# A decode step bound by its loads: one row block of the last weight matrix loaded first of all

## The chip, the cores and the metric

The kernel runs on one core of one Trainium2 chip. The metric is the device time of one execution in microseconds (us); lower is better. Names used below: PE is the matrix engine (TensorE), DVE the vector engine, ACT the scalar engine, POOL the general one (GpSimd), SP the engine that issues nearly all DMAs here.

## The reference

One token goes through a block of attention over a long key and value cache and then through a mixing and feed-forward block.

```
x  [1,1,512], wq [512,4096], k_cache, v_cache [1,8,16384,128], wo [4096,512]
w1, w2 [512,512], w3 [512,1792], w4 [1792,512]

h  = x + A(layernorm(x), k_cache, v_cache, wq, wo)
     A: q = x @ wq as 32 heads of 128, four heads to each of 8 key heads
        p = softmax(q k^T / sqrt(128)),  o = p v,  result = o @ wo
out = h + B(layernorm(h), w1, w2, w3, w4)
     B: h1 = gelu(layernorm(x) @ w1); its four quarters are shifted along the
        sequence by +1, -1, +2, -2 with zeros shifted in; hs = shifted @ w2
        x1 = x + hs
        result = x1 + gelu(layernorm(x1) @ w3) @ w4
```

The sequence has one position, so each shift leaves zeros only: hs is zero, w1 and w2 do not matter, and the kernel does not load them. Everything is bfloat16.

## The kernel before

All that the kernel reads is streamed from HBM once, 79 MB, by DMAs that SP issues one after another on one queue (line 458, the helper `load`). The order is: the query weights wq (4 MB, into the buffer vb), the first two halves of the keys (4 MB each, into the two halves of kb), the values of the first pair (8 MB, into vb), and then for three more pairs of key heads the two key halves and the values. Then come wo in two pieces (`WO`, blocks 0 to 20 and 20 to 32), w3 in one (`W3`) and w4 in three (`W4`). A buffer is loaded again as soon as its last reader is done: SP waits for the transposes of the keys (DVE, line 635) or for the matmuls with the values (PE, line 686), and then issues. Only the tiny load of x goes by ACT's queue.

The start: x is normalised (lines 579 to 602); DVE's cast xn (line 603) also waits for wq; 32 matmuls (line 612) make the queries; DVE spreads them (lines 619 and 626). The first value load waits for these matmuls, since it overwrites wq.

Each of the four pairs of key heads: DVE transposes both key halves into kt (line 635), PE multiplies them with the queries (line 646), DVE and ACT do the softmax (lines 660 to 675), PE multiplies with the values (line 686), DVE and PE gather the result (lines 702 to 710). While the softmax runs, PE is given matmuls that nobody reads (line 498).

The end: the product with wo (line 755), the sum with x and its row sums (lines 767, 512 to 524), the product with w3 (line 780), the gelu in two halves on ACT (line 792), two transposes on DVE that lay its result out as hcol (line 796), and the product with w4 (line 803). w4 is [1792, 512]; the kernel sees it as 14 row blocks, block m being rows m, 14+m, 28+m and so on over 128 partitions, 512 columns (1 KB) to a partition, so a block is 128 KB. For each block PE does four matmuls of 128 columns, 56 in all, into one accumulator. The pieces are blocks 0 to 7, 8 to 12, and 13 alone. The first matmul that needs a piece waits for it, except that the wait for the first piece is put on the first transpose of line 796. The first half of hcol holds blocks 0 to 6, the second blocks 7 to 13. DVE and ACT then copy one half of the result each (lines 810 and 811), and SP stores it (line 813).

The order of work on each engine is the order in which the program is written; nothing reorders it. Between engines, a class that records every operation (lines 25 to 89) works out from the tiles read and written which semaphore each operation waits for.

Of the kernel before, what the change touches and what calls it, by code (L numbers as in the profile page):

```python
# [7 lines left out]
BF16 = mybir.dt.bfloat16  # L8
# [333 lines left out]
D = 512  # L342
# [8 lines left out]
NHC = FM // 128  # L351
# [2 lines left out]

SEEN, ROUND = 47, 28
W3 = ((0, 4),)
W4 = ((0, 8), (8, 13), (13, 14))
PAIRS = HKV // 2
RPARTS = 6
QPAD = 4 * 7  # L360
# [10 lines left out]
def bass_sequential_preLN__gqa_block_cached__mixer_s_mlp__decode_kernel(  # L371
# [13 lines left out]
    with ExitStack() as ctx:  # L385
        sb = lambda name, shape, dt: ctx.enter_context(nc.sbuf_tensor(name, shape, dt))
# [50 lines left out]
        hg = sb("hg", [128, FQ], BF16)  # L437
        hT = sb("hT", [128, NCH, 32], FP32)
        hcol = sb("hcol", [128, NHC, 32], BF16)
        fin = sb("fin", [64, 256], BF16)  # L440
        kb_all = sb("kb", [128, 256 * DH], BF16)
        kb = [kb_all[:, i * 128 * DH:(i + 1) * 128 * DH] for i in range(2)]
# [4 lines left out]
        w4_sb = kb[1][:, NCH * FM:2 * NCH * FM].rearrange("p (m c) -> p m c", m=NHC)  # L447
# [9 lines left out]
        def load(name, dst, src, key, by="SP", also=()):  # L457
            P.op(by, lambda e: e.dma_start(dst, src), w=[key, *also], dma=name)  # L458
# [33 lines left out]
        def pe(fn, r=(), w=(), bank=(), also=(), times=None, many=1):  # L492

            return P.op("PE", fn, r, w, bank, also=also, times=times, many=many)
# [6 lines left out]
        def piece(cuts, m):  # L501
            return [lo <= m < hi for lo, hi in cuts].index(True)
# [42 lines left out]
        def inverse_roots(i, ns):  # L545
# [9 lines left out]
            for m in range(3):  # L555
# [5 lines left out]
                else:  # L561
# [2 lines left out]
                        r=[(S, 8)], w=[(T, k + n) for k in (0, 2) for n in ns])  # L564


        load("x4", x4[:, :], A_x[0, 0:1, :].rearrange("o (q j) -> (o q) j", q=4), "x4", "ACT")
        load("wq", wq_sb[:, 0:NCH * HQ * DH], A_wq.rearrange("(p k) c -> p (k c)", k=NCH), ("v", 0), also=[("v", x) for x in range(1, VP)])
        load_keys(0, 0)
# [10 lines left out]
            r=["ident_f", "x4"], w=["quarter"])  # L580
        pe(lambda e: e.matmul(O_ps[0][:, 0:128], quarter[:, :, :].rearrange("p q u -> p (q u)"), x4[:, :],  # L581
                              start=True, stop=True), r=["quarter"], w=[("O", 0)], bank=[("O", 0)])
# [9 lines left out]
            r=["ident_f"], w=["row32"])  # L592
        dve(lambda e: e.tensor_reduce(maskdd[:, :], ident_f[:, :].rearrange("p (n d) -> p d n", d=4), AX.X, ALU.add),
            r=["ident_f"], w=["maskdd"])
# [3 lines left out]
        for z, src, key, of, n in ((zo, row32[:, :].rearrange("p (g n h) -> p g h n", g=2, h=REP), "zo", "row32", 4),  # L598
# [6 lines left out]
            r=["hT", (("st", 0), 0), (("st", 0), 6)] + [("v", x) for x in range(VP)], w=["xn"])  # L605
# [3 lines left out]
        for i, key in enumerate(keys):  # L609
            P.part("query", i)  # L610
            for k in range(NCH):
                pe(lambda e, k=k: e.matmul(row[:, bass.ds(P.b + P.b0, 512)], copies(xn[:, k:k + 1], 128),  # L612
                                           wq_k[:, k, bass.ds(P.c + P.c0, REP * DH)], start=(k == 0), stop=(k == NCH - 1)),
                   r=["xn"], also=[("v", x) for x in range(VP)], w=["n" if key == "mn" else key], bank=[key])
        P.part()
        for g in range(2):
            half = banks[64 * g:64 * g + 64, PAIRS * g:PAIRS * g + PAIRS, :].rearrange("p j c -> p (j c)")
            for b in range(2):
# [3 lines left out]
                    r=["n" if x == "mn" else x for x in keys[PAIRS * g:PAIRS * g + PAIRS]], w=["qcol"],  # L622
# [118 lines left out]
        w3_in = B_w3.rearrange("(p k) f -> p k f", p=128)  # L741
        for n, (lo, hi) in enumerate(W3):
            load(f"w3{n}", w3_sb[:, lo:hi, :], w3_in[:, lo:hi, :], ("r", 1, n))
        w4_in = B_w4.rearrange("(p m) c -> p m c", p=128)
        for n, (lo, hi) in enumerate(W4):
            load(f"w4{n}", w4_sb[:, lo:hi, :], w4_in[:, lo:hi, :], ("r", 1, len(W3) + n))

# [2 lines left out]
            r=["o_m"], w=["o_f"])  # L750
        dve(lambda e: e.tensor_copy(o_b[:, :], o_f[:, :]), r=["o_f", ("r", 0, 0)], w=["o_b"])  # L751

        for r_ in range(32):
# [3 lines left out]
                                              stop=(r_ < 4 or r_ >= 28), skip_group_check=(r_ >= 4)),  # L757
               r=["o_b"] + [("r", 0, n) for n in (piece(WO, r_),) if n], w=[("O", 0)], bank=[("O", 0)],
# [3 lines left out]
        h_ps, hkey = banks[:, 6, :], "spare0"  # L762
        for n in range(2):
            dve(lambda e, n=n: e.tensor_copy(osum[:, 256 * n:256 * n + 256], O_ps[0][:, 256 * n:256 * n + 256]),
                r=[("O", 0)], w=[("osum", n)], bank=[("O", 0)])
        for q in range(4):
            pe(lambda e, q=q: e.matmul(h_ps[32 * q:32 * q + 32, 0:128], copies(row32[:, 0:1], 32),
                                       osum[:, q * 128:(q + 1) * 128], start=True, stop=True),
               r=[("osum", q // 2), "row32"], w=[hkey], bank=[hkey])
# [4 lines left out]
            r=["hT", (S, 0)] + [("r", 1, 0)], w=["hc"])  # L774
# [3 lines left out]
        for k in range(NCH):  # L778
            for q in range(4):
                pe(lambda e, k=k, q=q: e.matmul(s_ps[32 * q:32 * q + 32, 0, 0:FQ], hc[:, k, :],  # L780
                                                w3_sb[:, k, q * FQ:(q + 1) * FQ], start=(k == 0), stop=(k == NCH - 1)),
                   r=["hc"] + [("r", 1, n) for n in (piece(W3, k),) if n], w=[("s", 0)], bank=[("s", 0)])
# [6 lines left out]
            r=["xs", (S, 6), "hr"], w=[hkey], bank=[hkey])  # L789
        for n in range(2):  # L790
# [5 lines left out]
            dve(lambda e, lo=lo, hi=hi: e.transpose(  # L796
                hcol[:, lo:hi, :].rearrange("p m u -> p (m u)"),
                hg[:, :].rearrange("p (i m) -> p m i", m=NHC)[:, lo:hi, :]), r=[("hg", n)] + [("r", 1, len(W3))] * (n == 0), w=[("hcol", n)])
        for m in range(NHC):
            if m == 4:  # L800
                pe(None)
            for o in range(4):
                pe(lambda e, m=m, o=o: e.matmul(
                    h_ps[32 * o:32 * o + 32, 0:128], hcol[:, m, :], w4_sb[:, m, o * 128:(o + 1) * 128],
                    start=False, stop=(m == NHC - 1), skip_group_check=True),
                   r=[("hcol", 2 * m // NHC)] + [("r", 1, len(W3) + n) for n in (piece(W4, m),) if n],
                   w=[hkey], bank=[hkey])


# [5 lines left out]
             r=[("fin", 0), ("fin", 1)], w=["out"], dma="out")  # L815
# [32 lines left out]
```

## Time and profile before

| What | Value |
|---|---|
| Median of 3 runs | 189.83 us (189.8 to 189.89) |
| The profiled execution | 189.74 us |
| Its span, first to last instruction | 188.4 us |
| PE, DVE busy | 127.9 us (68%), 116.8 us (62%) |
| ACT, POOL busy | 13.7 us (7%), 4.6 us (2%) |
| SP's DMA queue, share of the 16 engines' span | 97.9% |
| Bytes read from HBM | 79.17 MB, 420 GB/s over the span |

Durations below come from the profiled execution. Its time is the span and some 1.3 us around it. How to read the rows: the profile's page has a line for each resource with the span cut into 40 equal slices, a digit giving the busy share in tenths. In a timeline a row is start, duration, engine, line, operation, tiles and shape, number of instructions, and in brackets the idle time before it and what ended that. In a table of windows, each engine has its busy time and in brackets how many of its instructions touch the window; the last three columns are the granted PE clock, the DMA engines' busy share and GB/s. A DMA packet is counted in the window in which it starts. SP's rows give only the issuing; when a load lands is told by the table of issues, as time from issue to landing.

### The profile page before, as it was taken

How to read it: one execution, taken by the hardware profiler on the slowest of the kernel's cores; microseconds unless marked ns; L12 is line 12 of the kernel's file. 1: busy time of each engine (PE TensorE's matmuls, PEld its weight loads, DVE VectorE, ACT ScalarE, POOL GpSimd, SP SyncE). 2: the span in 40 equal slices, each digit the busy share in tenths (PEclk: the TensorE clock that was granted, in tenths of full speed). 3: DMA queues.
4: the chain of work that ended last, by engine and by line, in shares of the span. 5: the costliest groups of instructions: out<-in, count | busy, mean ns of one | idle time of the engine just before them, and what ended most of it. 6: DMA issues, size and time to landing. Idle time of an engine off the chain costs nothing.

```text
span 188.4 us, 2405 instructions
## 1 busy us (share of the span) xinstructions
PE 127.9 (68%) x767; PEld 49.6 (26%) x767; DVE 116.8 (62%) x139; ACT 13.7 (7%) x21; POOL 4.6 (2%) x8
## 2 busy tenths in 40 slices
PE   0109705979699059796980697969829997885772
PEld 0104201423225024232240242322413332222221
DVE  5740799795451897944518979445279897513173
ACT  3000200000040000000400000003000000500012
POOL 8100000000000000000000000000000000000000
PEclk9999985899999859999998599999988999999999
DMA  6999999999799999999999999997999989899994
GB/s 223 445 445 445 445 417 473 445 445 445 334 445 445 445 501 417 390 390 417 445 445 445 445 445 445 445 445 334 445 445 445 556 390 417 362 393 424 435 411 177
DMA packets 2751, 79.19 MB, mean 420 GB/s; under 512 B 318, under 2 KB 446, under 8 KB 574
## 3 DMA queue, kind: packets, MB, share of 16 engines
q1 hardware_dynamic: 2742, 79.17, 97.9%
q8 instruction: 1, 0.02, 0.0%
q10 hardware_dynamic: 8, 0.00, 0.0%
HBM read 79.17 MB, written 0.00 MB: 420 GB/s over the span
## 4 chain that ended last, share of the span: by engine, by line
DMA 36%; DVE 29%; PE 29%; issue 4%; SPq 0%; DVEq 0%
DVE kt L635 24%; DMA kb<-in_A_k_cache_dram 15%; DMA kb<-in_B_w_dram 15%; PE banks L646 13%; DMA vb<-in_A_wq_dram 7%; PE banks L498 6%; PE banks L612 5%; PE banks L686 4%; DVE mx L660 1%; DVE od L705 1%; DVE qcol L619 1%; PE banks L663 1%; PE banks L708 0%; SPq L458 0%; DVE od L702 0%
## 5 line engine op out<-in xcount | busy, mean ns | idle before, releaser
L646 PE MATMUL banks<-kt,qn 128*128 x256 | 68.8, 409 | 26.8 <-DVE kt L635 26.0
L635 DVE STREAM_TRANSPOSE kt<-kb 128x4096 int32<-128x4096 int32 (+2 forms) x25 | 70.7, 2878 | 5.4 <-PE banks L646 4.0
L646 PEld LDWEIGHTS banks<-kt,qn 128*128 x256 | 26.0, 102 | 69.1 <-issue 53.1
L498 PE MATMUL banks<-qb 128*128 128x512 bf16 x70 | 25.5, 388 | 0.6
L686 PE MATMUL banks<-vb,pt 128*32 128x512 bf16 x256 | 14.7, 379 | 0.9 <-POOLq L480 0.9
L671 ACT ACTIVATE p_sb<-banks,bias 128x1024 bf16<-128x1024 f32 x4 | 4.5, 1114 | 132.7 <-DVE nmh L667 132.7
L660 DVE TENSOR_REDUCE mx<-banks 128x1 f32<-128x1024 f32 x4 | 4.9, 1225 | 14.2 <-PE banks L646 14.2
L675 DVE STREAM_TRANSPOSE pt<-p_sb 64x1024 bf16<-64x1024 bf16 x8 | 9.9, 1239 | 5.4 <-ACT p_sb L671 5.3
L612 PE MATMUL banks<-vb,xn 128*128 x32 | 8.6, 436 | 6.8 <-DVE xn L603 6.8
L498 PEld LDWEIGHTS banks<-qb 128*128 128x128 bf16 x70 | 6.7, 97 | 18.3 <-issue 18.1
L702 DVE TENSOR_SCALAR od<-banks,rowc 128x128 f32<-128x128 f32 x4 | 1.4, 351 | 14.4 <-PE banks L686 14.4
L686 PEld LDWEIGHTS banks<-vb,pt 128*32 128x32 bf16 x256 | 8.5, 97 | 5.1 <-POOLq L480 1.0
L619 DVE STREAM_TRANSPOSE qcol<-banks 64x1024 f32<-64x1024 f32 x4 | 4.8, 1227 | 6.8 <-PE banks L612 6.8
L612 PEld LDWEIGHTS banks<-vb,xn 128*128 128x128 bf16 x32 | 3.5, 110 | 11.4 <-issue 8.7
L663 PE MATMUL banks<-mxd,mean 128*128 128x128 f32 x8 | 2.0, 326 | 6.6 <-DVE mxd L661 6.6
L708 PE MATMUL banks<-od,zo 128*32 128x128 f32 x8 | 1.6, 285 | 6.5 <-DVE od L705 6.5
L655 ACT ACTIVATE banks<-mean 128x1024 f32<-128x1024 f32 x4 | 4.1, 1027 | 18.7 <-DVE qcol L619 18.6
L695 DVE RECIPROCAL den<-banks 32x1 f32<-32x1 f32 x4 | 0.6, 156 | 6.9 <-PE banks L693 6.9
L705 DVE SCALAR_TENSOR_TENSOR od<-banks,rowc,od 128x128 f32<-128x128 f32 x12 | 4.2, 351 | 0.4
L755 PE MATMUL banks<-kb,o_b 128*32 128x512 bf16 x44 | 3.3, 384 | 1.6 <-DVE o_b L751 1.1
L581 PE MATMUL banks<-x,quarter 4*128 4x128 bf16 x1 | 0.3, 283 | 5.5 <-DVE quarter L579 5.5
L579 DVE CAST quarter<-ident_f 4x128 bf16<-4x128 f32 x1 | 3.2, 3224 | 1.0 <-DMA x<-in_A_x_dram 1.0
(69 smaller groups left out, 39.6 us busy)
## 6 DMA issues: line engine op xcount, KB each, us to landing
kb<-in_A_k_cache_dram SPq DMA_DIRECT2D x8, 4096.0 KB, 27.8
vb<-in_A_wq_dram SPq DMA_DIRECT2D x1, 4096.0 KB, 12.3
kb<-in_A_wo_dram SPq DMA_DIRECT2D x1, 2560.0 KB, 26.1
kb<-in_B_w_dram SPq DMA_DIRECT2D x1, 1792.0 KB, 24.2
kb<-in_A_wo_dram SPq DMA_DIRECT2D x1, 1536.0 KB, 29.4
kb<-in_B_w_dram SPq DMA_DIRECT2D x1, 1024.0 KB, 26.3
kb<-in_B_w_dram SPq DMA_DIRECT2D x1, 640.0 KB, 27.4
kb<-in_B_w_dram SPq DMA_DIRECT2D x1, 128.0 KB, 27.3
```

What stands on the lines that cost most here:

```text
L498: P.op("PE", lambda e: e.matmul(O_ps[1][:, :], field[:, 0:128], field[:, 0:512], start=True, stop=True), r=["qb"], bank=[("O", 1)], times= ...
L612: pe(lambda e, k=k: e.matmul(row[:, bass.ds(P.b + P.b0, 512)], copies(xn[:, k:k + 1], 128), wq_k[:, k, bass.ds(P.c + P.c0, REP * DH)], sta ...
L619: dve(lambda e, g=g, b=b, half=half: e.transpose(qcol[64 * g:64 * g + 64, 2 * b:2 * b + 2, :, :].rearrange("p e m u -> p (e m u)"), half.r ...
L635: P.op("DVE", lambda e, view=view: e.transpose(view(kt), view(kb[y])), r=[("r", y, i) for i in range(RPARTS)], w=[("kt", t + i) for i in r ...
L646: pe(lambda e, n=n: e.matmul(row[:, bass.ds(P.y, 512)], qn[:, n, bass.ds(P.q, 128)], key_piece(P.k, n), start=False, stop=(n == 3), skip_g ...
L655: act(lambda e: e.activation(s_all, copies(mean4[:, 0:1], 1024), ACTF.Identity, scale=0.0), r=["mean4", "p"], w=[("s", 0), ("s", 1)], **both)
L660: dve(lambda e: e.tensor_reduce(mx[:, :], s_all, AX.X, ALU.max), r=[("s", 0), ("s", 1)], w=["mx"], **both)
L663: pe(lambda e: e.matmul(m_ps[:, 0:128], mean4[:, :], mxd[:, :], start=True, stop=True), r=["mxd", "mean4"], w=["m"], bank=["mn"])
L671: act(lambda e: e.activation(p_sb[:, :], s_all, ACTF.Exp, bias=bias[:, 0:1], scale=float(SCALE), accum_out=acc[:, :]), r=[("s", 0), ("s", ...
L675: dve(lambda e, g=g: e.transpose(pt[64 * g:64 * g + 64, :, :, g, :], p_sb[64 * g:64 * g + 64, :]), r=["p"], w=["pt"])
L686: pe(lambda e, l=l, ct=ct, ch=ch: e.matmul(O_ps[0][32 * ct:32 * ct + 32, :], pt[:, l, ch, :, :].rearrange("p g u -> p (g u)"), tiles[:, l ...
L705: dve(lambda e, block=block, c=c: e.scalar_tensor_tensor(od[:, :], block, rowc[:, c:c + 1], od[:, :], ALU.mult, ALU.add), r=[key, "rowc", ...
```

## The change

Block 13 of w4 gets a tile of its own, w4e, and is loaded by SP's first DMA, ahead of wq. The three pieces at the end now hold blocks 0 to 7, 8 to 11, and 12. PE takes the blocks in the order 0 to 6, 13, 7 to 12; the matmuls of block 13 read w4e and wait for its load. The total of bytes is the same; there is one DMA more, and SBUF holds 1 KB more on each partition, ahead of the buffers fin, kb, vb and kt.

```diff
-W4 = ((0, 8), (8, 13), (13, 14))
+W4 = ((0, 8), (8, 12), (12, 13))
+M4 = (*range(7), 13, *range(7, 13))
...
+        w4_e = sb("w4e", [128, D], BF16)
...
+        w4_in = B_w4.rearrange("(p m) c -> p m c", p=128)
+        load("w4e", w4_e[:, :], w4_in[:, 13, :], "w4e")
         load("x4", x4[:, :], A_x[0, 0:1, :].rearrange("o (q j) -> (o q) j", q=4), "x4", "ACT")
         load("wq", wq_sb[:, 0:NCH * HQ * DH], A_wq.rearrange("(p k) c -> p (k c)", k=NCH), ("v", 0), also=[("v", x) for x in range(1, VP)])
...
-        w4_in = B_w4.rearrange("(p m) c -> p m c", p=128)
...
-        for m in range(NHC):
-            if m == 4:
+        for n, m in enumerate(M4):
+            if n == 4:
                 pe(None)
             for o in range(4):
                 pe(lambda e, m=m, o=o: e.matmul(
-                    h_ps[32 * o:32 * o + 32, 0:128], hcol[:, m, :], w4_sb[:, m, o * 128:(o + 1) * 128],
-                    start=False, stop=(m == NHC - 1), skip_group_check=True),
-                   r=[("hcol", 2 * m // NHC)] + [("r", 1, len(W3) + n) for n in (piece(W4, m),) if n],
+                    h_ps[32 * o:32 * o + 32, 0:128], hcol[:, m, :],
+                    (w4_e[:, :] if m == 13 else w4_sb[:, m, :])[:, o * 128:(o + 1) * 128],
+                    start=False, stop=(m == M4[-1]), skip_group_check=True),
+                   r=[("hcol", 2 * m // NHC)] + (["w4e"] if m == 13 else
+                                                 [("r", 1, len(W3) + i) for i in (piece(W4, m),) if i]),
                    w=[hkey], bank=[hkey])
```

## The prediction

> **What bounds the kernel now.** I read the page from the bottom of the machine upwards: first the slices and the queue table, then the tail of the timeline, then the stretch in which the loads begin.
>
> ```profile
> DMA  6999999999799999999999999997999989899994
> GB/s 223 445 445 445 445 417 473 445 445 445 334 445 445 445 501 417 390 390 417 445 445 445 445 445 445 445 445 334 445 445 445 556 390 417 362 393 424 435 411 177
> ...
> q1 hardware_dynamic: 2742, 79.17, 97.9%
> ```
>
> SP's queue q1 keeps the sixteen DMA engines occupied for 97.9% of the span. The two slices with a 7 are no idle time: a packet counts where it starts, and the neighbours of 334 GB/s carry 473 and 501 or 556. So the loads form one stream from the first slice to the last, in the order in which SP issues them. Does the computing ever hold that stream up? In the timeline of DVE, no:
>
> ```profile
> 139.08 8.95 DVE L635 STREAM_TRANSPOSE kt<-kb 128x1024 int32<-128x1024 int32 x5 [0.63 <-DMA kb<-in_A_k_cache_dram]
> 148.80 1.25 DVE L635 STREAM_TRANSPOSE kt<-kb 128x1024 int32<-128x1024 int32 x1 [0.77 <-DMA kb<-in_A_k_cache_dram]
> ```
>
> In the last pair it is the key transposes that wait for keys, by 0.63 and 0.77 us. And every load is issued long before its turn: the page's table of issues shows medians of 24 to 30 us from issue to landing for all loads of weights, keys and values but the first. The tail of the timeline shows what ends last:
>
> ```profile
> 184.79 1.05 DVE L796 STREAM_TRANSPOSE hcol<-hg 128x224 bf16<-128x224 bf16 x2 [0.80 <-DMA kb<-in_B_w_dram]
> 185.42 0.71 PE L803 MATMUL banks<-kb,hcol 128*32 128x128 bf16 x32 [1.75 <-DVE hcol L796]
> 186.33 0.55 PE L803 MATMUL banks<-kb,hcol 128*32 128x128 bf16 x24 [0.19 <-DMA kb<-in_B_w_dram]
> 186.93 0.28 DVE L810 CAST fin<-banks 64x128 bf16<-64x128 f32 x1 [1.09 <-PE banks L803]
> 187.28 0.32 SPq L813 DMA_DIRECT2D out_dram<-fin  x1
> ```
>
> The 24 matmuls from 186.33 are row blocks 8 to 13. Blocks 8 to 12 wait for the 640 KB piece, which the chain of waits lands at 186.28. Block 13 waits for the last 128 KB: issued at 159.32 and landed 27.3 us later, at 186.6. Counting the L803 matmuls by window:
>
> ```profile
> 186.30:186.59 0.29, 0.26 (x20) 0.27 (x20) 1.00 0.23 56
> ```
>
> The second field in brackets is the number of matmuls: 20 of the 24 have begun by 186.59, so the last four begin after the last landing. The end hangs on that landing, not on the number of matmuls ahead of it. Call its time L (186.6).
>
> **The change, part by part.**
>
> *The tail loses one block, worth 0.32 us of stream.* From issue plus time to landing, the last pieces land at 182.2 (1792 KB), 184.7 (1024 KB), 186.28 (640 KB) and 186.6 (128 KB). That is 2.5 us for eight blocks, 1.6 for five, 0.32 for one: 0.31 to 0.32 us a block, whatever the piece. The middle piece with four blocks takes 1.28. The last piece is as large as before, so the stream after the query weights ends 0.32 us earlier relative to its own beginning.
>
> *One more DMA.* A block costs 0.307 us in the 1792 KB piece, 0.303 in a key load (4096 KB, 22.7 to 32.4, 9.7 us) and 0.32 alone. So a block in a DMA of its own costs at most 0.02 more. I add 0.02. The SP issue itself is priced next.
>
> *The head gains one block.* SP's first issues:
>
> ```profile
> 0.74 0.40 SPq L458 DMA_DIRECT2D vb<-in_A_wq_dram  x1
> 1.19 0.42 SPq L458 DMA_DIRECT2D kb<-in_A_k_cache_dram  x1
> ```
>
> One issue takes SP from 0.74 to 1.19, a step of 0.45 us. The new load takes the first place and the query weights (wq) the second, at 1.19; both key loads move back a step too, and wait in the queue anyway. What is unknown is how much later wq's bytes flow. From one side: w4e's bytes go through the same engines first, 0.32 us. From the other: if start-up runs from wq's own issue, wq moves by the whole step, 0.45, and the engines idle for 0.13 us between the two, since 128 KB lasts less than a step. I take the middle, 0.39, because both rows bear on it equally. Ends further apart are the rivals.
>
> The Trainium skill's "DMA: Bandwidth & Descriptors" speaks against a load as small as this: in its section on why a DMA increments its semaphore by 16, a table gives 2 KiB per partition as the least that saturates the DMAs on earlier generations, and the new load has 1 KiB. By that rule I estimate the queue would run dry for as long again as the load lasts, and the sum would be 190.17. The trace neither shows nor excludes it: its only 1 KiB load lies at the tail, behind a full queue.
>
> *What waits for wq.* The cast xn (L603) waits 1.9 us for it now, and the query matmuls, the first transposes and the first value load (issued at 22.52) all move by 0.39. The value load has cover: the second key load lands at 32.4, so it waits in the queue for 10 us. DVE's chain reaches the last pair 0.39 later; the two waits of 0.63 and 0.77 absorb that, all the more as the keys land later too. Without this cover the price would be the 0.39.
>
> *The matmul order.* Block 13 moves ahead of block 7: still 56 matmuls on PE. It reads the second half of hcol, as block 7 does, and a load that landed 180 us before; the added wait is on something long done, and behind it stand block 7 and the rest of L803. Is there room? The first piece now lands 1.60 before L (it was 1.92). Transposes start 0.10 later and take 1.05, so hcol is ready at L-0.45, and PE goes on at L-0.41. In the window 185.40 to 185.85 PE begins 28 matmuls, 0.4 us, so a block is 0.06: blocks 13 and 7 end at L-0.29. The four-block piece lands at L-0.32 and is seen 0.04 later (186.28 to 186.33); 16 matmuls take 0.23, to L-0.05. The last four can start at L+0.04. So the landing still ends last, with 0.09 to spare, and four fewer matmuls after the middle piece gain nothing: they had been done before L already.
>
> *The sum.* +0.39 at the head, -0.32 at the tail, +0.02 for one more DMA: +0.09 us, and with both ends of the head +0.02 to +0.15. The profiled execution took 189.74 (its span of 188.4 and 1.3 around it), so it would become 189.83. It lies 0.09 below the median 189.83, to which I refer the forecast: **189.92**.
>
> **The rivals.**
>
> *Hidden in the start-up, 189.53.* The windows of the first loads, with the DMA columns last:
>
> ```profile
> 1.75:2.25 0.50, 0.00 (x0) 0.00 (x0) 0.08 (x1) 0.50 (x1) 0.50 (x1) 1.00 3.26 852
> 2.25:3.50 1.25, 0.00 (x0) 0.00 (x0) 1.25 (x1) 0.55 (x2) 1.25 (x1) 1.00 0.24 79
> 3.50:4.25 0.75, 0.00 (x0) 0.00 (x0) 0.75 (x1) 0.00 (x0) 0.75 (x2) 1.00 1.61 699
> 4.25:4.75 0.50, 0.00 (x0) 0.00 (x0) 0.50 (x1) 0.00 (x0) 0.50 (x1) 1.00 0.00 0
> ```
>
> GB/s times length gives bytes started: 426 KB and 99 KB, then 524 KB. In packets of 32 KB that is 13 and 3 first ones, then 16 second ones. The third round starts 1.25 after the second, but the second about 1.85 after the first: the first round takes some 0.6 us too long, and all sixteen second packets begin within 0.75 us though the first ones began over a longer stretch. If that surplus is a fixed time in which the engines cannot yet flow, w4e passes within it, wq is not delayed, and the time is 189.83 - 0.32 + 0.02. Against it: wq must still be issued 0.45 later.
>
> *Start-up paid twice, 190.45 (the slower side).* If each engine's first transfers from a new load pay the surplus whenever nothing is in flight, w4e pays 0.6 plus its 0.32, the engines run dry, and wq pays its own again. wq moves by 0.92: +0.92 - 0.32 + 0.02 = +0.62. It needs the dry gap of 0.13; it is slower by over 0.2% as soon as wq lands more than 0.68 us later, after 13.7. Against it: later loads, which follow on a full queue, show no such surplus.
>
> *A longer dry gap, 190.17.* If two blocks' worth of transfer (0.64) would be needed to bridge to wq, it moves by 0.64: +0.64 - 0.32 + 0.02 = +0.34. For it: SP's step is 0.45, but 1.0 us pass from an issue at 0.74 to the first packets after 1.75. Against it: issues overlap with that delay. The rule cited above gives the same figure.
>
> *It does not do what it says.* The order of SP's queue and of the matmuls in the built program is as written, so only the gain could be missing: that is the forecast itself.
>
> **How the numbers follow.** The forecast (189.85 to 189.98) gets 0.62, hidden 0.15, longer gap 0.08, paid twice 0.11, and 0.04 is left for what I do not see, half on each side. The range 189.50 to 190.25 takes in the forecast, the longer gap and most of hidden (0.11), in all 0.81. This kernel's measurement tells about 0.2% (0.38 us) from no change. Faster by more: 0.04 of hidden, should the tail save a little too, and 0.02: 0.06. Slower by more: paid twice, 0.03 of the longer gap and 0.02: 0.16. Within: 0.78.
>
> **What would show it.** wq should land at 13.3 to 13.45 (now 13.00); first key load, last value load and first w4 piece later by the same 0.32 to 0.45 plus at most 0.02; the last landing at 186.6 to 186.75; the last four matmuls 0.04 behind it; 1.8 us from there to the end of the span, as now. Hidden would show wq at 13.0 and the last landing at 186.3; paid twice, wq after 13.7 and a stretch without packets near 2.3. I would be wrong about the tail if the last four matmuls began without a wait for their load, and about the cover if a load began with its queue empty.

## The result, and the profile after

| | Before | After |
|---|---|---|
| Median (runs) | 189.79 us (11) | 190.25 us (11) |
| Lowest and highest | 189.61, 189.89 | 189.85, 190.54 |
| Profiled execution | 189.74 us | 190.28 us |
| Span, mean granted PE clock | 188.4 us, 0.934 | 189.0 us, 0.919 |

The ratio is 1.0022 (95%: 1.0014 to 1.0030), and the medians are 0.46 us apart: a little more than the 0.2% that this measurement can tell. The forecast was 189.92; the time lies on the upper end of its range, 190.25.

The page of after, the same rows as before, with the row of the clock ahead of them and the shares of the chain of waits behind:

```profile
PEclk9999985599999965999999669999996999999789
DMA  7999999999799999999999999997999998989993
...
q1 hardware_dynamic: 2886, 79.17, 97.7%
...
PE 51%; DVE 35%; DMA 6%; issue 6%; ACT 0%; SPq 0%; DVEq 0%; ACTq 0%
```

The queue is as full as it was (97.7% against 97.9%). But the chain of waits that ended last is now almost wholly computing; before, loads had 36% of it. The clock row and the shares of before, for comparison:

```profile
PEclk9999985899999859999998599999988999999999
...
DMA 36%; DVE 29%; PE 29%; issue 4%; SPq 0%; DVEq 0%
```

The dips come in turn with the pairs of key heads in both. After has one more, the digits 7 and 8 near the end of its row (177.1 to 180.5 us); in before the clock stayed up there.

**The loads did what was forecast.** SP's first issues in after:

```profile
0.73 0.40 SPq L460 DMA_DIRECT2D w4e<-in_B_w_dram  x1
1.18 0.42 SPq L460 DMA_DIRECT2D vb<-in_A_wq_dram  x1
```

And the table of windows over the first packets:

```profile
1.75:2.25 0.50, 0.00 (x0) 0.00 (x0) 0.07 (x1) 0.50 (x1) 0.50 (x1) 1.00 0.76 170
2.25:3.50 1.25, 0.00 (x0) 0.00 (x0) 1.25 (x1) 0.55 (x2) 1.25 (x1) 1.00 1.62 456
3.50:4.25 0.75, 0.00 (x0) 0.00 (x0) 0.75 (x1) 0.00 (x0) 0.75 (x2) 1.00 0.51 218
4.25:4.75 0.50, 0.00 (x0) 0.00 (x0) 0.50 (x1) 0.00 (x0) 0.50 (x1) 1.00 1.67 721
```

GB/s times length: 85 KB start before 2.25, all of them w4e's. The next window has the rest of w4e and the first sixteen packets of wq, 570 KB. The second sixteen packets of wq, 524 KB, start between 3.50 and 4.75; in before they had all started by 4.25. From issue plus time to landing:

| Landing, us | Before | After |
|---|---|---|
| w4e | | 2.96 |
| wq | 13.00 | 13.43 |
| Last values | 168.11 | 168.54 |
| w4, first and middle piece | 184.69, 186.28 | 185.12, 186.39 |
| w4, last piece | 186.60 | 186.71 |

From wq to the first piece of w4 everything is 0.43 later. From wq to the last landing before took 173.60 and after 173.28, less by 0.32. The last landing is 0.11 later.

**The computing did not.** In after's timeline DVE's transposes of the last pair's keys are one uninterrupted row:

```profile
141.34 17.95 DVE L639 STREAM_TRANSPOSE kt<-kb 128x1024 int32<-128x1024 int32 x13
```

There is no wait in brackets where before had two, 0.63 and 0.77. DVE begins this pair 2.26 later than before (141.34 against 139.08), so it no longer waits for keys but runs behind them. The delay begins at the query matmuls: they start 0.43 later and end 1.77 later. First before, then after:

```profile
13.82 8.59 PE L612 MATMUL banks<-vb,xn 128*128 x32 [6.77 <-DVE xn L603]
```

```profile
14.24 9.94 PE L616 MATMUL banks<-vb,xn 128*128 x32 [7.20 <-DVE xn L607]
```

The same 32 matmuls take 1.35 us more. They follow each other by 0.43 us at the low clock and by 0.22 at the high one, and the clock rose at 16.91 in before, at 20.07 in after.

Most of this delay is taken up further on, by a wait that the prediction did not name. In the last pair PE works off 16 matmuls that nobody reads while the softmax runs, and then turns to the last values. First before, then after:

```profile
161.10 6.00 PE L498 MATMUL banks<-qb 128*128 128x512 bf16 x16
168.21 3.64 PE L686 MATMUL banks<-vb,pt 128*32 128x512 bf16 x64 [0.90 <-POOLq L480]
```

```profile
162.89 6.00 PE L500 MATMUL banks<-qb 128*128 128x512 bf16 x16
168.89 0.40 PE L690 MATMUL banks<-vb,pt 128*32 128x512 bf16 x3
```

In before the matmuls start 0.09 us after the last values land (168.11), though the bracket names POOL, and so they do, by 0.09 to 0.10, in all the other traces of this document but two. In after the matmuls that nobody reads end only at 168.89, 0.35 after the landing (168.54). So of the delay 0.26 is left here. The other exception is e6 below, with 0.63.

At the other end the product with wo, before and after:

```profile
174.92 2.55 PE L755 MATMUL banks<-kb,o_b 128*32 128x512 bf16 x32 [1.05 <-DVE o_b L751]
177.95 0.83 PE L755 MATMUL banks<-kb,o_b 128*32 128x512 bf16 x12 [0.48 <-DMA kb<-in_A_wo_dram]
```

```profile
175.67 4.73 PE L758 MATMUL banks<-kb,o_b 128*32 128x512 bf16 x44 [1.05 <-DVE o_b L754]
```

Before waited 0.48 for the second piece of wo. After waits for no load; it starts 0.75 later and ends at 180.40 instead of 178.78. The window shows why it is slow (the third column from the right is the granted clock):

```profile
177.00:180.40 3.40, 3.40 (x32) 1.12 (x34) 0.00 (x0) 0.00 (x0) 0.00 (x0) 0.51 0.99 419
```

The tail follows from that:

```profile
185.74 1.05 DVE L799 STREAM_TRANSPOSE hcol<-hg 128x224 bf16<-128x224 bf16 x2
186.37 0.57 PE L806 MATMUL banks<-kb,hcol 128*32 128x128 bf16 x28 [1.54 <-DVE hcol L799]
186.84 0.24 PE L806 MATMUL banks<-w4e,hcol 128*32 128x128 bf16 x4
186.91 0.51 PE L806 MATMUL banks<-kb,hcol 128*32 128x128 bf16 x24
187.47 0.28 DVE L815 CAST fin<-banks 64x128 bf16<-64x128 f32 x1 [0.68 <-PE banks L806]
```

The transposes had no load to wait for (before: 0.80), nor had the last 24 matmuls (before: 0.19). The transposes begin 0.95 later than in before: 0.43 for the later landing of the last values, 0.26 for PE's late start behind it, and 0.27 by which the slower product with wo and the steps behind it exceed before's wait of 0.80. The last four matmuls began at 187.19, 0.48 after their load. In before, and in the second trace of after below, the time is the last landing plus 3.14 us. By that measure these loads would have allowed 189.85, which is what the shortest runs of after take; this execution took 190.28. The measure is good to some 0.1: in the second trace of before it is 3.25.

### The profile page after: what moved, and what is told of

Same layout as the page of the kernel before. It is cut to its first block, busy times and chain, and to the rows that moved or that the text cites. A ratio compares the mean times of both kernels' runs of the same rounds, so it can differ in the third digit from the quotient of the medians.

```text
span 189.0 us, 2406 instructions
## 1 busy us (share of the span) xinstructions
PE 131.1 (69%) x766; PEld 51.1 (27%) x767; DVE 116.6 (62%) x139; ACT 13.7 (7%) x21; POOL 4.6 (2%) x8
## 3 DMA queue, kind: packets, MB, share of 16 engines
q1 hardware_dynamic: 2886, 79.17, 97.7%
## 4 chain that ended last, share of the span: by engine, by line
PE 51%; DVE 35%; DMA 6%; issue 6%; ACT 0%; SPq 0%; DVEq 0%; ACTq 0%
DVE kt L639 25%; PE banks L650 20%; PE banks L500 12%; PE banks L690 8%; DMA vb<-in_A_wq_dram 6%; PE banks L616 5%; DVE mx L664 3%; PE banks L758 2%; DVE od L709 2%; PE banks L667 1%; PE banks L712 1%; DVE od L706 1%; DVE qcol L623 1%; DVE mxd L665 1%; PE banks L806 1%
## 5 line engine op out<-in xcount | busy, mean ns | idle before, releaser
L650 PE MATMUL banks<-kt,qn 128*128 x256 | 70.0, 416 | 25.6 <-DVE kt L639 25.5
L616 PE MATMUL banks<-vb,xn 128*128 x32 | 9.9, 487 | 7.2 <-DVE xn L607 7.2
L690 PEld LDWEIGHTS banks<-vb,pt 128*32 128x32 bf16 x256 | 9.2, 97 | 3.5
L758 PE MATMUL banks<-kb,o_b 128*32 128x512 bf16 x44 | 4.7, 552 | 1.1 <-DVE o_b L754 1.1
```

The costliest lines, as they stand in the source:

```text
L650: pe(lambda e, n=n: e.matmul(row[:, bass.ds(P.y, 512)], qn[:, n, bass.ds(P.q, 128)], key_piece(P.k, n), start=False, stop=(n == 3), skip_g ...
L690: pe(lambda e, l=l, ct=ct, ch=ch: e.matmul(O_ps[0][32 * ct:32 * ct + 32, :], pt[:, l, ch, :, :].rearrange("p g u -> p (g u)"), tiles[:, l ...
L758: pe(lambda e, r_=r_, q=q: e.matmul(O_ps[0][32 * q:32 * q + 32, :], copies(o_b[:, r_:r_ + 1], 32), wo_sb[:, r_ * D:(r_ + 1) * D], start=(r ...
```

## The experiments

Two theories. **Clock:** the loads cost +0.11, and the rest is computing that comes late, because a later start of the query matmuls meets the periods of PE's clock differently. **Cover:** the computing from the landing of the last values to the end takes nearly as long as the loads behind them, and in after these take 18.17 us instead of 18.49. The expectations also speak of a load theory (only the loads count), a tail theory (the order of the blocks, the added wait and the smaller pieces cost the time) and, from e4 on, a placement theory. A kernel's time stands beside the median of before on the same chip (189.72 for e0 to e3, 189.81 for a0 and e4 to e6, 189.74 for e7 to e10).

**Before and after once more.** Before, unchanged:

> The kernel before, unchanged, to see how far its compute chain moves from run to run beside loads that stand still. Clock theory (the later start of the query matmuls lets PE miss a period of full clock, the computing then comes too late for the last loads): the median is again 189.8, the last landing near 186.6; where PE's clock rises after the query start may differ from the earlier trace, and the computing may end a little before or after the last landing. Load theory (only the stream of loads has moved): last landing and time the same as in the earlier trace within 0.1.

Measured: 189.82 (189.68 to 189.95, 11 runs), 1.0004 (0.9995 to 1.0013). Its trace is worth as much as the time:

```profile
168.18 5.32 PE L686 MATMUL banks<-vb,pt 128*32 128x512 bf16 x64 [0.88 <-POOLq L480]
...
185.05 1.05 DVE L796 STREAM_TRANSPOSE hcol<-hg 128x224 bf16<-128x224 bf16 x2
```

The clock rose at 18.18, not 16.91; the matmuls with the last values ran in large part at half clock (5.32 us instead of 3.64); the product with wo ended at 179.70, not 178.78. The transposes into hcol waited for no load, and the last four matmuls began at 186.61, 0.04 after the last landing. So before has little slack in its computing too, and the trace that I predicted from showed more than there commonly is. After, unchanged:

> The changed kernel once more, for a second trace and more times. Clock theory: again 190.0 to 190.5 with a wide spread; the loads end at 186.7 as in its first trace, but the place where PE's clock rises in the query matmuls and falls in the product with wo is another one, and the computing ends after the last landing by as much as that costs. Load theory: wq at 13.4, last landing at 186.7, the last matmuls directly behind it.

Measured: 190.26 (189.86 to 190.60, 11 runs), 1.0025 (1.0016 to 1.0034). The profiled execution is one of the short ones, 189.90:

```profile
175.40 4.49 PE L758 MATMUL banks<-kb,o_b 128*32 128x512 bf16 x44 [1.05 <-DVE o_b L754]
...
185.26 1.05 DVE L799 STREAM_TRANSPOSE hcol<-hg 128x224 bf16<-128x224 bf16 x2 [0.15 <-ACT hg L795]
...
186.43 0.60 PE L806 MATMUL banks<-kb,hcol 128*32 128x128 bf16 x24
187.09 0.28 DVE L815 CAST fin<-banks 64x128 bf16<-64x128 f32 x1 [0.78 <-PE banks L806]
```

Here hcol comes 0.48 earlier than in the first trace of after, and the last landing (186.76) decides again: the last four matmuls begin at 186.80, as the prediction had it. The same program ends by its loads in one execution and by its computing in another, and its runs spread over 0.7 us.

**The block loaded at another place.** The matmuls and the pieces of the tail are as in after; only the load moves: behind wq (e1, shown), or behind the last values, ahead of wo (e7, the same line further down).

```diff
-        load("w4e", w4_e[:, :], w4_in[:, 13, :], "w4e")
         load("x4", ...)
         load("wq", ...)
...
+        load("w4e", w4_e[:, :], w4_in[:, 13, :], "w4e")   # e1: here
         load_keys(0, 0)
```

> The changed kernel with the early block loaded second, behind the query weights, instead of first: wq lands as early as in the kernel before, all else as changed. Clock theory: the query matmuls start at 13.8 again, the computing is back in time, and the kernel takes 189.8 (ratio to before 0.999 to 1.001). Tail theory (the new order of the blocks and its added wait cost the time): still 190.1 to 190.3.

> The changed kernel with the separate block loaded behind the last values and ahead of wo, instead of first of all: nothing ahead of the last values is later than in the kernel before. Cover theory (every load but the last two pieces lands 0.43 later in the changed kernel, and the computing from the landing of the last values to the end is nearly as long as the 18.5 us that the loads behind them take, so it now ends after the last landing): 189.7 to 189.85, as the kernel before. Tail theory (block order, extra wait, smaller pieces): 190.0 or more.

Measured: e1 189.88 (189.72 to 190.57, 11 runs), 1.0012 (1.0002 to 1.0021), with wq at 12.93 and the last landing at 186.56. e7 189.78 (189.75 to 190.44, 11 runs), 1.0008 (0.9999 to 1.0017), with the last landing at 186.57. Most of the loss goes with the place: 8 of the 11 runs of e1 and 8 of the 11 of e7 took 189.90 or less, but only 3 of the 22 of after. The intervals are wide, though: e1's overlaps with after's, and e7's allows a loss of up to 0.32 us. In e7 the order of the matmuls, the wait for w4e, the pieces of 8, 4 and 1, the extra DMA and the moved buffers are all there, and no loss can be told. That speaks against the tail theory. The profiled execution of e7 is one of two long ones among its runs, 190.38:

```profile
185.70:187.50 1.80, 1.68 (x56) 1.41 (x56) 0.49 (x2) 0.06 (x1) 0.00 (x0) 0.52 0.08 27
```

The clock fell at 185.77 and was low for the last 56 matmuls (0.52), which took 1.68 us instead of 1.05 to 1.2. The computing was not late here: hcol was begun at 185.08, as in before again, but the copy of the result started 0.87 after the last landing instead of 0.33. That is a second way to a run half a microsecond longer, and it occurs with the head untouched.

**Each half of the change alone.** The tail alone (e9): block 13 is not loaded, its matmuls read block 12 instead. The head alone (e10): before, with block 13 loaded first of all into a tile that nobody reads, and once more at the end.

```diff
e9
-W4 = ((0, 8), (8, 13), (13, 14))
+W4 = ((0, 8), (8, 12), (12, 13))
...
-w4_sb[:, m, o * 128:(o + 1) * 128]
+w4_sb[:, min(m, 12), o * 128:(o + 1) * 128]
e10
+        w4_e = sb("w4e", [128, D], BF16)
...
+        load("w4e", w4_e[:, :], B_w4.rearrange("(p m) c -> p m c", p=128)[:, 13, :], "w4e")
         load("x4", ...)
```

> The kernel before with the last two pieces of w4 as in the changed one (four blocks, one block), block 13 not loaded at all, its matmuls reading block 12 in its place: a stream shorter by 128 KB at its end, the head untouched, PE's work the same. Load theory: the last landing comes 0.32 earlier, 186.28, and the time with it, 189.45. Cover theory: the computing behind the last values does not fit into 18.2 us in part of the runs, so less than 0.32 is gained: 189.55 to 189.7, with a wider spread.

> The kernel before with block 13 loaded first of all into a tile that nothing reads, and loaded again at the end as ever: the head of the change without its tail. Both theories: every load lands 0.43 later, the last at 187.0, and as the cover is unchanged the time goes up by that, to 190.2, with the spread of the kernel before. Then the changed kernel (190.25) has from its shorter tail next to nothing.

Measured: e9 189.49 (189.38 to 189.68, 11 runs), 0.9987 (0.9978 to 0.9996): 0.25 gained of the 0.32 that the stream is shorter. Its profiled execution, 189.68, the longest of its runs, is bound by computing: the product with wo takes 4.73 us, and the 56 last matmuls run in one go, the last four 0.18 after the last landing (186.40):

```profile
185.76 1.05 PE L803 MATMUL banks<-kb,hcol 128*32 128x128 bf16 x56 [1.55 <-DVE hcol L796]
```

e10 190.52 (190.16 to 190.62, 5 runs), 1.0044 (1.0030 to 1.0057): 0.78 lost, which no theory expected. Its trace, of the shortest run (190.16), shows the loads as they should be: wq at 13.36, the last landing at 187.01, 0.41 later than in the first trace of before. Here the landing decides:

```profile
186.09 1.21 PE L805 MATMUL banks<-kb,hcol 128*32 128x128 bf16 x56 [1.55 <-DVE hcol L798]
```

The last four matmuls begin at 187.06, 0.05 after it. The other four runs, 190.40 to 190.62, were not profiled. The two halves sum to 0.53, near the change's 0.46. So the tail gives back nearly what it should, and the head costs up to twice what it does to the loads. The cover theory needs the shorter tail, and e10 loses more with the tail of before, so it cannot be the whole. It does show in e9: from the landing of the last values to the copy of the result the computing took 18.64 us, where the loads allowed 18.51.

**The query matmuls delayed alone.** Before, with a small reduction on DVE ahead of the cast xn, whose result nobody uses. In e2 it writes to a new tile of 160 bytes on each partition, in e6 to a part of an existing one; e4 has the new tile and nothing else.

```diff
e2 and e4
+        pad = sb("pad", [128, 40], FP32)
...
e2 (e6: osum[:, 0:40] in place of pad[:, :])
+        dve(lambda e: e.tensor_reduce(pad[:, :], mean4[:, 0:40].unsqueeze(2).to_broadcast([128, 40, 5]), AX.X, ALU.add),
+            r=["mean4"] + [("v", x) for x in range(VP)], w=["pad"])
```

> The kernel before with all its loads as they were, and one extra DVE instruction of about 0.4 us between the landing of wq and the cast xn (its result is not used). Clock theory: the query matmuls start 0.4 later, and the time goes up to 189.95 to 190.3 although the last landing stays at 186.6. Load theory: nothing happens, 189.8, since the waits of 0.63 and 0.77 in the last pair absorb 0.4.

Measured: 189.31 (189.08 to 189.93, 11 runs), 0.9984 (0.9973 to 0.9994): faster, against all theories. The last landing came at 186.04. The new tile moves the buffers behind it by 160 bytes, which mixes two edits. Hence e4 and e6:

> The kernel before with a tile of 160 bytes per partition that nothing uses, allocated where the extra tile of the delay experiment lay; it moves the load buffers by 160 bytes. Placement theory (the delay experiment was faster because its buffers lay elsewhere: its 32 KB packets took 1213 ns each where those of the kernel before took 1213 to 1221): 189.2 to 189.4, last landing near 186.0. If the delay itself had made it faster: 189.8.

> The kernel before with an extra DVE instruction of about 0.4 us between the landing of wq and the cast xn, written into a tile that exists already, so that no buffer moves (its result is not used). Clock theory: 189.9 to 190.2, with a wider spread than before, although all loads land as before. Load theory: 189.75, nothing to see.

Measured: e4 189.31 (189.06 to 189.68, 11 runs), 0.9976 (0.9967 to 0.9985), the last landing at 185.97. From wq to the last landing it takes 173.03 instead of 173.60. The page:

```profile
span 187.8 us, 2405 instructions
...
DMA packets 2751, 79.19 MB, mean 422 GB/s; under 512 B 318, under 2 KB 446, under 8 KB 574
```

The packets are as many as in before, and as large; before's page has 420 GB/s. Nine in ten packets of 32 KB take 1213 ns, in before 1213 to 1221. It beats both kernels, and has nothing to do with the change: after, whose buffers are moved by 1 KB, has the rate of before (173.28 and the 0.32 that it lacks).

e6, free of that: 189.82 (189.69 to 190.03, 11 runs), 1.0000 (0.9991 to 1.0009). The query matmuls start some 0.28 later against wq's landing, not the 0.4 intended (the change has 0.43), and the median doesn't move; the clock theory had expected 189.9 to 190.2 and misses. The long runs may be more: 4 of the 11 took 189.97 or more, against 4 of 33 of before on the same chip. The profiled execution (190.02) does show its chain:

```profile
186.11 1.05 PE L805 MATMUL banks<-kb,hcol 128*32 128x128 bf16 x56 [1.54 <-DVE hcol L798]
```

56 matmuls in one go, not held up by the last landing at 186.50, after a product with wo of 4.72 us. But that is one execution, at the upper end of its runs.

**The clock raised ahead of the query.** After, with matmuls that nobody reads ahead of the query: 14 written out (e3), or 17 by a loop (e5; its expectation says 18).

```diff
e3
+        for _ in range(14):
+            unread(None)
e5
+        nc.switch_bb("pe_warm", parent=None)
+        ops[lo - 1].fn(eng)
+        eng.reg_add(ry, ry, 1)
+        eng.br_lt(ry, 16, "pe_warm", "pe_warmed")
```

> The changed kernel with 14 more matmuls that nobody reads, on PE between the first row sums and the query matmuls, so that PE is busy when wq lands. Clock theory: the query matmuls run at 0.22 us each from the start (7 us in all instead of 9.9), the computing is early again, and only the loads decide: 189.9. Load theory and tail theory: still 190.2.

> The changed kernel with 18 matmuls that nobody reads, as a loop of few instructions, on PE up to the start of the query matmuls. Clock theory: the 32 query matmuls take some 7 us instead of 9.9, all computing comes 2 us earlier, and only the loads decide: 189.8 to 189.9 with a small spread. Load theory and tail theory: 190.2 as without them.

Measured: e3 193.13 (193.09 to 193.46, 5 runs), 1.0185 (1.0171 to 1.0199), for a reason of its own:

```profile
186.44 0.46 PE L808 MATMUL banks<-kb,hcol 128*32 128x128 bf16 x17
189.87 0.40 PE L808 MATMUL banks<-kb,hcol 128*32 128x128 bf16 x7 [2.98 <-issue]
```

PE stops for 2.98 us in the midst of its last matmuls, for nothing that the profile shows ("issue"), with every load landed. The 14 matmuls written out are all that was added. What PE waited for is not shown. Nor did it test what it should: the unread matmuls ended at 12.09, the clock fell again at 14.41, and the query took 8.76. e5 189.99 (189.76 to 190.58, 11 runs), 1.0014 (1.0005 to 1.0023), with the query at 7.8 us: 0.18 above before where after has 0.45. It has 17 matmuls more, and its interval overlaps with after's, so this is a hint that the clock has part in it, no proof. Its profiled run is a long one, 190.42, and yet its computing was in time: hcol waited 0.39 for its load. As in e7 the clock fell late (185.63), the last 56 matmuls took 1.69 us, and the copy started 0.86 after the last landing (186.65).

**PE kept busy ahead of the product with wo.** After, with four unread matmuls on top of each gather, to keep the clock up:

```diff
+            unread(4)
```

> The changed kernel with a loop of four more matmuls that nobody reads ahead of the last matmul of each pair's gather, where PE waits for DVE anyway, so that PE's clock falls less often to half in the product with wo. Cover theory: the product with wo takes 3.1 to 3.9 us instead of 4.5 to 4.7, the computing ends before the last landing, and the time goes to 189.85 to 189.95 with a narrower spread. If the loads alone made the changed kernel slower: 190.2 as it is.

Measured: 190.06 (189.89 to 190.84, 11 runs), 1.0025 (1.0015 to 1.0036). It did not do what it was for: the clock still fell at 176.41, and the product with wo took 4.66. It doesn't decide between the theories.

## Why the prediction came out as it did, point by point

- **The tail loses one block: −0.32.** Right. From wq to the last landing, 173.28 instead of 173.60. One more DMA, set at +0.02, cannot be told from 0.
- **The head gains one block: +0.39, between 0.32 and 0.45.** Right: wq +0.43, near the end at which wq moves by SP's whole issue step (0.45). Over all traces wq lands at 13.36 to 13.50 with the block loaded first, and at 12.91 to 13.06 without. The sum for the last landing, +0.09, measured +0.11, and +0.19 between the second traces.
- **The matmul order, the added wait and the first value load: nothing.** Right. With the load placed late, all of the tail's edits together cost 0.04 at the median, which is not told from none (e7). SP issued the first value load 1.77 later (24.29 instead of 22.52), still 8 us ahead of its turn, and the queue stayed at 97.7%.
- **The rivals.** Hidden (wq at 13.0) and paid twice (after 13.7) are excluded by wq at 13.43; the longer gap would have put wq at 13.64. The Trainium skill's table in "DMA: Bandwidth & Descriptors" (why a DMA increments its semaphore by 16) gives 2 KiB per partition as the least that saturates the DMAs on earlier generations; with 1 KiB, the estimate was a dry time as long as the load. The trace doesn't bear that out here: of wq's 0.43, the load's own transfer is 0.32, and 0.11 is left for a gap.
- **"DVE's chain reaches the last pair 0.39 later; the two waits of 0.63 and 0.77 absorb that."** This step failed: it put the cost of the head to the computing at nothing. In the trace of after the query matmuls ended 1.77 later, DVE reached the last pair 2.26 later, and both waits were gone. A third wait, PE's for the last values, took up all but 0.26 of that, and in the second trace of after all of it; the rest of the cover, hcol's wait of 0.80, went to the slower product with wo. I had moved the computing of one trace by 0.39 as a rigid block. Between two traces of before, 189.74 and 189.82, it differs by about as much as the slack: hcol began with a wait of 0.80 for its load in the one and with none in the other. The sign that I had named for a failing cover, a load that begins with its queue empty, did not appear; it was the wrong sign, as the cover failed at the end of the computing and not in the queue.
- **"So the landing still ends last, with 0.09 to spare."** This follows from the step above and holds in some runs only: in the second trace of after (0.04 from landing to matmuls), not in the first (0.48). The sign that the prediction had named for this, last matmuls without a wait for their load, is what the first trace shows.
- **What the clock has to do with it.** The traces of before, before again, after, and after again have the rise at 16.91, 18.18, 20.07 and 19.00, that is 3.1 to 5.8 us behind the first query matmul. All later changes of a trace lie whole multiples of 3.41 us behind that rise. In "TensorE: Matmul & The Clock Gate", Part 1, the Trainium skill says that the clock is judged over windows of 3413 ns that run freely and do not start with the kernel. The traces agree on the step of 3.41, and on a phase that differs from execution to execution. So how much of the query and of the wo product runs at half clock differs from run to run. The mean granted clock of the trace that I used, 0.934, occurs in 5 of 98 runs of before and in none of 22 of after, whose highest is 0.928. I took a rare trace, the one with the wo product at full clock, for the rule. But the mean clock does not tell a run's time: those five runs of before took 189.65 to 189.81, the runs of after at 0.919 took 189.85 to 190.60, and e10's one run at 0.934 took 190.40.
- **The range.** That 190.25 still lies on the end of the range is luck. Its upper part was there for a longer dry gap at the head, which the traces exclude. A loss of more than 0.2% had a chance of 0.16, nearly all of it for loads that come later than they did.

How much of the 0.46 is explained: 0.11 by the loads in the first traces, 0.19 in the second ones. For the rest, two ways are on record, and neither is shown to be the whole.

One is computing that ends behind the loads. Where the loads decide, the copy of the result starts 0.33 to 0.34 after the last landing; it started 0.76 after it in the first trace of after, 0.72 in e6, 0.46 in e9 and 0.41 in e8. By this way alone the longest runs are not reached. From the first query matmul to hcol the longest stretch in any trace is 171.49 us, from there to the copy 1.73, and from the copy to the time of the run 2.81 to 2.95. My estimate from these is that late computing takes after to 190.35 to 190.49 at most, and e10 to 190.21 to 190.35. Four of the five runs of e10 took 190.40 to 190.62.

The other is the clock that falls on the last matmuls, as in e7 and e5, which adds some 0.53. It needs no change at the head. Whether the long runs of after and e10 are of this kind, no trace shows; the longest that were profiled are 190.28 and 190.16.

Over all runs the tenth from the bottom rises from 189.64 to 189.87, the median from 189.75 to 190.26, the tenth from the top from 189.94 to 190.51 (98 runs of before, 22 of after). So the runs also spread further, as they would by either way. What stays open is why the head costs that much. A later query alone costs nothing at the median (e6), later loads alone should cost 0.43, and both together cost 0.78 (e10, 95%: 0.57 to 1.08 by its ratio). The place at the head is shown as the cause (after and after again against e1 and e7, and e10); the way by which it acts beyond the loads is argued from few traces, and the phase of the clock could not be set by hand to prove it.

## What to carry to other kernels

In a stream that is full from end to end, moving a block to the front moves the cost and does not remove it: here the block took 0.43 us at the head and gave back 0.32 at the tail. Only a transfer that fits into idle time could win; no run here tried one. When the loads are the bound, ask how far behind the computing ends, and ask it of several traces: the slack of 0.80 us in the one that I used was gone in the next trace of the same kernel. And follow a delay through every later wait, for loads as for other engines, before you call it absorbed or lost.

## What the runs showed of the hardware that I had not expected

- An unused tile of 160 bytes ahead of the load buffers made the whole kernel 0.24% faster (e4, 0.9976, 0.9967 to 0.9985): the stream from wq on took 0.57 us less. Why is not shown.
- 28 more instructions on PE (14 matmuls and their weight loads) brought a stall of 2.98 us near the end of the program (e3); a loop that runs more matmuls brought none (e5). Why is not shown.
- The half clock can fall on the last matmuls: 56 of them took 1.68 us in a window at 0.52 (e7), 1.05 at full clock (e9). The copy of the result then started 0.87 after the last landing instead of 0.33.
